# A Conformer block on one core: the sum of the attention output's halves in one reduce or in two, and other constants for the planner

## The chip, the core and the metric

The kernel runs on one core of a Trainium2 chip. Times are device microseconds of one execution of the whole program. Its engines work side by side, each through its own list of instructions in order: PE (matrix multiplies, with PEld for the weight loads), DVE (vector work), ACT (functions such as exp), POOL (small vector work) and SP (issues DMAs). PSUM, where PE writes, has 8 banks of 512 float32 for each of 128 partitions.

## What is computed

Two sequences of 4000 rows of 144 go through one Conformer block: a feed-forward half step, attention with 4 heads of 36, a gated convolution of 5 taps, a second feed-forward half step, and layer norms. The part that matters here is the attention:

```python
qkv = h @ w_qkv                                  # B, T = 2, 4000; 4 heads of 36
scores = jnp.einsum('bhqd,bhkd->bhqk', q, k) * scale
p = _softmax(scores, axis=-1)
att = jnp.einsum('bhqk,bhkd->bhqd', p, v)
att = att.transpose(0, 2, 1, 3).reshape(B, T, D)
x = x + att @ w_o
```

The softmax is taken without a maximum: the exps are summed along with the product with v, by a column of ones beside v, and the division comes at the end.

## The kernel before

**Tiles.** Queries are cut into chunks of 512 (the eighth of each sequence has 416), heads into two pairs. A chunk with a pair of heads is a group; there are 2 x 8 x 2 = 32, in a fixed order. In a group, keys come in 31 tiles of 128 and a rest of 32. For one tile of keys PE computes the scores of both heads into two PSUM banks (tile PS<-QT,KT, four matmuls of 64 x 64 by 512), ACT takes the exp of both in one instruction of 128 x 1024 (PT<-PS), and PE multiplies it with v into banks 4 and 5 (PS<-PT,VA, four matmuls): the upper 64 keys of the tile add up in bank 4, the lower 64 in bank 5. So at the end of a group the attention output lies in two halves that have to be added. The scores use banks 0 to 3 in turn; banks 6 and 7 serve all other work.

**Exp on DVE.** Since ACT is the busiest engine, some exps are computed on DVE by bits: one instruction per head takes the scores from PSUM to an integer that is nearly the exp's bit pattern (PU<-PS), and four more over both heads correct it (`exact`: PF<-PU, PC<-PF, PC<-PC,PF, PU<-PU,PC). Either a whole tile goes this way (`far_tiles`: taken from the far end of the group's list of key tiles, or of the next group's), or one head of a tile goes to ACT and the other to DVE (`emit_exp`, a split tile). PU has 3 buffers (`NPD`), PT has 7 (`NPT`). The outputs of a DVE tile can only be added once its group is the current one and has begun.

**The end of a group.** When the last output matmul of a group is emitted, `output_done` starts `epilogue`. It adds the halves with one DVE tensor_reduce of banks 4 and 5 into OTF (128 x 512 float32), transposes OTF in four pieces of 128 queries on PE into one bank of 6 and 7 (PS<-IDF,OTF), takes the reciprocal of the sums (RD) and multiplies (AN). After the second pair of heads `post1` goes on with the output projection, the convolution and so on. The next group's first output matmul overwrites banks 4 and 5, and so waits for the reduce.

**The order.** There is no fixed schedule in the code. A planner (`Rec`, `Sched`) runs when the kernel is built: it keeps a modelled time for each engine, and each piece of work is a generator that asks for an engine with `need(...)`. `Sched.best` takes the request that can start first by the model; among those within a small window it takes the lowest rank (`free_first` is -1). A request's earliest time is the modelled end of the generator's last instruction, plus the latency `LAT` of its engine (`Sched.advance`, line 260). An instruction that a generator emits without a `need` in front of it comes straight after the one before. The main loop at line 1237 emits scores (`emit_S`), exps (`emit_exp`) and outputs (`emit_pending`); outputs whose exp is not ready, or whose group has not become the current one, are held in a list, and no new scores are emitted when six are held.

**The order constants** stand in `TUNE` (line 342): eight tuples for eight stretches of four groups each. By position: (0) how long after ACT could start may DVE come free for a tile to be split; (1) a far tile is taken from a group only while more than so many key tiles are left in it; (2) how long before POOL comes free the correcting DVE instructions may be planned (`Quiet`); (3) the window in `Sched.best`; (4) with how many tiles left the corrections are hurried.

Of the kernel before, what the change touches and what calls it, by code (L numbers as in the profile page):

```python
# [6 lines left out]
ALU = mybir.AluOpType  # L7
# [30 lines left out]
class Rec:  # L38
# [2 lines left out]


    ENGS = ("pe", "act", "dve", "pool", "sp")
    LAT = dict(pe=0.195, act=0.243, dve=0.152, pool=0.08, sp=3.0)
    NEAR = {("act", "dve"): 0.06, ("dve", "dve"): 0.028, ("pool", "dve"): 0.04}

    def __init__(self, nc):
# [11 lines left out]
    def op(self, eng, name, *a, r=(), w=(), q=None, cost=0.1, kind=None, lat=None, port=False, **k):  # L59
        o = Op()  # L60
        o.eng, o.name, o.a, o.k, o.q = eng, name, a, k, q
        o.deps, o.inc, o.cnt = [], False, 0
        lane = eng if q is None else "q:" + q
        o.idx = self.n.get(lane, 0)
        self.n[lane] = o.idx + 1
        for key in r:
            h = self.hist.setdefault(key, ([], []))
            o.deps += [(d, True) for d in h[0]]
            h[1].append(o)
        for key in w:  # L70
            h = self.hist.setdefault(key, ([], []))
            o.deps += [(d, False) for d in h[0] + h[1] if d is not o]
            if h[1] and not (len(h[1]) == 1 and h[1][0] is o):
                self.hist[key] = ([o], [])
            else:
                h[0].append(o)
        start = self.free[eng]
        for d, raw in o.deps:
            if d.eng != eng or d.q is not None or (raw and eng != "pe"):
                start = max(start, d.done - self.NEAR.get((d.eng, eng), 0.0))  # L80
        if eng == "pe":
            if kind != self.kind:
                start += 0.1
            self.kind = kind
        end = start + cost
        if eng == "pool" and self.run_end > end - 0.05:
            end = self.run_end + 0.13
        if port:
            self.run_end = end
            if self.behind is not None and start < self.free["pool"] - 0.05 < end:  # L90
                p, th = self.behind
                late = end + 0.13 - self.free["pool"]
                self.free["pool"] += late
                p.done += late
                if th is not None:
                    th.ready = max(th.ready, p.done)
        self.free[eng] = end
        o.done = end + (self.LAT[eng] if lat is None else lat) + (0.045 if kind == "q" else 0.0)
        self.last = o.done
        if eng == "pool":  # L100
            self.behind = (o, self.cur)
        self.ops.append(o)
        return o
# [119 lines left out]
def need(eng, slots=None, kids=(), cond=None, rank=None):  # L223
    return (eng, slots, kids, cond, rank)
# [76 lines left out]
def bass_standalone__conformer_family_zipformer__speech_kernel(  # L301
# [21 lines left out]
    def wid(c):  # L323
        return LAST if c % CPB == CPB - 1 else CH
# [4 lines left out]
    R = Rec(nc)  # L329
    op = R.op  # L330
    S = Sched(R)

    def sb(name, shape, dt=BF16):
        return nc.alloc_sbuf_tensor(name, [128] + list(shape), dt)
# [4 lines left out]
    GAP = 0.2  # L339
    MORE = 3  # L340
    HURRY, RELAX = -2, 1
    TUNE = [(0.003, 10, 0.47, 0.032, 3), (0.003, 10, 0.47, 0.032, 3), (0.003, 10, 0.47, 0.032, 3), (0.025, 10, 0.56, 0.065, 3), (0.089, 13, 0.66, 0.057, 3), (0.003, 10, 0.47, 0.032, 3), (0.022, 10, 0.67, 0.039, 3), (0.075, 12, 0.7, 0.063, 3)]
    LEAD = -2
    LAG, LAG_END = 5, 4
    NWARM = 30
# [4 lines left out]
    def tune(i):  # L350


        return TUNE[min(s_grp[0] * len(TUNE) // 32, len(TUNE) - 1)][i]

# [20 lines left out]
    OTF = sb("OTF", [CH], F32)  # L375
# [7 lines left out]
    IDF = sb("IDF", [128], F32)  # L383
# [22 lines left out]
    PSV = PS[:, :].rearrange("p (b n) -> p b n", n=512)  # L406
# [61 lines left out]
    for i in range(NWARM):  # L468
        op("pe", "matmul", PSV[:, i % 8, 0:256], lhsT=DUM[:, 0:128], rhs=DUM[:, :], start=True, stop=True,
           r=["DUM"], w=[("ps", i % 8)], cost=0.213 if i < 24 else 0.109)  # L470
# [51 lines left out]
    def dve_cost(n):  # L522
        return 0.07 + n / 960.0
# [298 lines left out]
    def post1(c, a):  # L822
        b, cc = c // CPB, c % CPB
        tb = wid(c) // NB
        s1 = yield need("pe", xtp)
        s2 = yield need("pe", xtp)

        def half(g):
            yield from transp(AN[0:tb, a, 2 * g:2 * g + 2, :], [("AN", a), "ANP"], c, s1, g)
            yield from residual(  # L830
                c, g, lambda i: [(xt(c, s1, k, i * tb, (i + 1) * tb), WO[0:KROWS[k], k, :]) for k in range(2)], 1.0,
                [("XT", s1, g), "WO"], 0.07)
            yield from ln_tr(c, s2, g)

        kids = S.spawn(half(g) for g in range(2))
        yield need("pe", kids=kids, cond=lambda: c < NUS or c - NUS in conv_done)
        xtp.give(s1)
        anp.give(a)
        kids = S.spawn([glu_a(c, s2), glu_b(c, s2)])
        yield need("pool", kids=kids)  # L840
        xtp.give(s2)
        us, up = c % NUS, (c - 1) % NUS
        if cc == 0:
            op("pool", "memset", UA[:, us, 2:4, 0:1], 0.0, w=[("UL", us)], cost=0.15)
            op("pool", "memset", UB[:, us, 0:1], 0.0, w=[("UL", us)], cost=0.15)
        else:
            for dst, src, w, r in (
                    (UA[:, us, 2:4, 0:1], UA[:, up, 2:4, TB:TB + 1], ("UL", us), ("U", up)),
                    (UB[:, us, 0:1], UB[:, up, TB:TB + 1], ("UL", us), ("U", up)),
                    (UA[:, up, 0:2, TB + 1:TB + 2], UA[:, us, 0:2, 1:2], ("UR", up), ("U", us)),  # L850
                    (UB[:, up, TB + 1:TB + 2], UB[:, us, 1:2], ("UR", up), ("U", us))):
                op("pool", "tensor_copy", dst, src, r=[r], w=[w], cost=0.25)
        if cc == CPB - 1:
            op("pool", "memset", UA[:, us, 0:2, tb + 1:tb + 2], 0.0, w=[("UR", us)], cost=0.15)
            op("pool", "memset", UB[:, us, tb + 1:tb + 2], 0.0, w=[("UR", us)], cost=0.15)
        glu_done.add(c)
# [72 lines left out]
            yield from g  # L929

    an_of = {}

    def epilogue(b, qc, p, gi):
        c = b * CPB + qc
        n, tb = wid(c), wid(c) // NB
        op("dve", "tensor_reduce", out=OTF[:, 0:n], in_=PSV[:, 4:6, 0:n].rearrange("p b n -> p n b"),
           axis=mybir.AxisListType.X, op=ALU.add, r=[("ps", 4), ("ps", 5)], w=["OTF"],
           cost=dve_cost(2 * n))
        bk = yield need("pe", banks)
        for i in range(NB):  # L940
            op("pe", "transpose", PSV[0:tb, bk, i * 128:(i + 1) * 128], OTF[:, i * tb:(i + 1) * tb],
               IDF[:, :], r=["OTF", "IDF"], w=[("ps", bk)], cost=0.122, kind="f")
        if p == 0:
            an_of[c] = yield need("dve", anp)
        yield need("dve", cond=lambda: c in an_of, rank=free_first)
        a = an_of[c]
        v = PSV[0:tb, bk, :].rearrange("p (i h d) -> p i h d", i=NB, h=2)
        op("dve", "reciprocal", RD[0:tb, gi % 2, :, :], v[:, :, :, DH], r=[("ps", bk)], w=[("RD", gi % 2)],
           cost=0.24)
        yield need("dve", rank=free_first)  # L950
        op("dve", "tensor_tensor",
           AN[0:tb, a, :, p * HD:(p + 1) * HD].rearrange("p i (h d) -> p i h d", h=2), v[:, :, :, 0:DH],
           RD[0:tb, gi % 2, :, :].rearrange("p i (h o) -> p i h o", o=1).to_broadcast([tb, NB, 2, DH]),
           op=ALU.mult, r=[("ps", bk), ("RD", gi % 2)], w=[("AN", a)], cost=0.38)
        banks.give(bk)
        if p == 1:
            yield from post1(c, a)
# [100 lines left out]
    def begun_group(gi):  # L1058
        return (gi, 4, 0) in begun or (gi, 4, 1) in begun
# [146 lines left out]
    while len(ff1_done) < CPB or 0 not in kv_done:  # L1206
        t, th = S.best()
        S.run(th)
    banks.restrict([6, 7])
    while banks.held - banks.only:  # L1210
        t, th = S.best()
# [12 lines left out]
    def emit_pending(force=False):  # L1224
        while pend:
            m = pend[0]
            gi = tiles[m][0]
            if gi != o_grp[0]:
                return
            t = exps[m]  # L1230
            if not begun_group(gi):
                t = max(t, R.ready("OTF"))
            if not force and len(pend) < NPT - 2 and t > R.free["pe"] + 0.1:
                return
            emit_O(pend.pop(0))

    while next_tile() is not None or n_e < len(tiles):
        a = s_start() if next_tile() is not None else R.free["pe"]
        full = len(pend) >= NPT - 1
        if full:  # L1240
            emit_pending(force=True)
            full = len(pend) >= NPT - 1
        t, th = S.best()
# [19 lines left out]
        if len(tiles) >= 2 or not more:  # L1263
            emit_exp(n_e)
            emit_pending()
            pend.append(n_e)
            n_e += 1
    while o_grp[0] < len(groups):
        emit_pending(force=True)
        if o_grp[0] < len(groups):  # L1270
            t, th = S.best()
# [7 lines left out]
    while S.threads:  # L1279
        t, th = S.best()  # L1280
# [34 lines left out]
```

## Time and profile before

| | |
|---|---|
| median of 3 unprofiled runs | 934.28 us (934.25 to 934.55) |
| profiled execution | 935.62 us |
| span of its instructions | 933.8 us |
| granted clock of PE | 1.00 throughout |
| HBM traffic | 3.31 MB read, 2.30 MB written |

The profile comes from one execution. Nearly all instructions carry line 163, the planner's helper that emits them, so they are told apart by their tiles: `PT<-PS` writes tile PT from PSUM. A group's row gives the busy time, the mean duration of one in ns, and the idle time of the engine just before them with what ended it. The first reduce of OTF starts at 82 us and the last at 897 us; before lies the first feed-forward part of the first sequence, behind lies what is left of the last chunk. The recorded durations of neighbouring instructions on one engine overlap a little, so where the time from one start to the next matters it is taken from the timeline.

### The profile page before, as it was taken

The page shows a single profiled execution, that of the slowest core. Times are in us where ns is not written, and L with a number is a line of the kernel's source. Part 1 is how long each engine was busy: PE and PEld are TensorE (multiplying, and loading weights), DVE is VectorE, ACT ScalarE, POOL GpSimd, SP SyncE. Part 2 cuts the span into 40 slices and gives each one's busy share as a digit, 9 for nine tenths or more (in the row PEclk, how much of TensorE's full clock was granted, in tenths as well). Part 3 has the DMA queues.
Part 4 walks back from the last instruction along what each step waited for, and adds up shares of the span by engine and source line. Part 5 has one row for each costly group of instructions (what it writes and reads, how often), then busy time and mean ns, then how long its engine had stood idle before and what let it go on. Part 6 is the DMA issues. An engine that isn't in the chain of part 4 may idle for free.

```text
span 933.8 us, 25544 instructions
## 1 busy us (share of the span) xinstructions
PE 860.8 (92%) x10838; PEld 343.0 (37%) x10838; DVE 858.4 (92%) x1975; ACT 884.2 (95%) x1126; POOL 170.8 (18%) x395
## 2 busy tenths in 40 slices
PE   8998899999999998999999999899988999899989
PEld 5633233333243333334343333333323333333447
DVE  8868999999999999999989999999999999898954
ACT  6799999999999999999999999999999999999963
POOL 7500010302111120211211111102202120130223
DMA  5310010103011020201100020101001020101100
GB/s 143 50 21 13 13 25 13 40 8 46 13 28 27 7 52 14 38 16 24 28 8 5 16 36 11 30 7 30 20 1 30 13 42 2 30 18 22 22 19 14
DMA packets 79810, 23.26 MB, mean 25 GB/s; under 512 B 77120, under 2 KB 79696, under 8 KB 79696
## 3 DMA queue, kind: packets, MB, share of 16 engines
q1 hardware_dynamic: 78656, 21.15, 11.6%
q8 instruction: 85, 1.39, 0.7%
q10 hardware_dynamic: 1040, 0.48, 0.2%
q14 instruction: 29, 0.24, 0.1%
HBM read 3.31 MB, written 2.30 MB: 6 GB/s over the span
## 4 chain that ended last, share of the span: by engine, by line
ACT 60%; PE 25%; DVE 13%; DMA 1%; issue 1%; POOL 1%; SPq 0%; ACTq 0%; DVEq 0%
ACT PT L163 52%; PE PS L163 25%; ACT TH L163 5%; DVE PU L163 4%; DVE PC L163 2%; DVE XN L163 1%; DVE ST L163 1%; DVE X L163 1%; ACT HT L163 1%; DVE HT L163 1%; DVE PF L163 1%; DVE OTF L163 1%; ACT PR L163 1%; DMA XT<-XN 0%; POOL RS L163 0%
## 5 line engine op out<-in xcount | busy, mean ns | idle before, releaser
L163 ACT ACTIVATE PT<-PS 128x1024 bf16<-128x1024 f32 (+2 forms) x848 | 795.8, 1067 | 9.7 <-PE PS L163 7.1
L163 PE MATMUL PS<-QT,KT 64*64 64x512 bf16 (+1 forms) x4032 | 431.1, 389 | 49.4 <-ACT PT L163 36.1
L163 PE MATMUL PS<-PT,VA 64*37 64x512 bf16 (+1 forms) x3350 | 327.1, 371 | 0.8 <-ACT PT L163 0.6
L163 PEld LDWEIGHTS PS<-QT,KT 64*64 64x64 bf16 x4032 | 128.2, 103 | 325.2 <-ACT PT L163 199.9
L163 DVE TENSOR_SCALAR PU<-PS 128x512 uint16<-128x512 f32 (+1 forms) x309 | 201.4, 671 | 5.8 <-PE PS L163 4.2
L163 POOL TENSOR_SCALAR RS<-ST 128x2 f32<-128x2 f32 (+1 forms) x160 | 33.2, 208 | 689.8 <-DVE ST L163 688.8
L163 POOL TENSOR_TENSOR RS<-RS,NHALF 128x2 f32<-128x2 f32 (+1 forms) x160 | 122.5, 766 | 13.3
L163 DVE TENSOR_TENSOR PC<-PC,PF 128x1024 bf16<-128x1024 bf16 (+1 forms) x155 | 103.4, 671 | 0.6
L163 DVE TENSOR_TENSOR PU<-PU,PC 128x1024 uint16<-128x1024 uint16 (+1 forms) x155 | 103.4, 669 | 0.2
L163 PEld LDWEIGHTS PS<-PT,VA 64*37 64x37 bf16 x3350 | 96.5, 96 | 13.5 <-ACT PT L163 1.3
L163 DVE TENSOR_SCALAR XN<-X,ST,RS 128x144 bf16<-128x144 bf16 (+1 forms) x312 | 83.2, 311 | 12.9 <-POOL RS L163 11.8
L163 ACT ACTIVATE TH<-PS 128x512 bf16<-128x512 f32 (+2 forms) x135 | 88.7, 657 | 1.9 <-PE PS L163 1.8
L163 PE MATMUL PS<-XT,WA 128*128 128x512 bf16 (+3 forms) x256 | 71.1, 378 | 6.7 <-DVE PU L163 3.4
L163 DVE BATCH_NORM_STATS2 ST<-X 128x6 f32<-128x288 bf16 (+1 forms) x160 | 69.1, 449 | 0.6 <-DMA X<-in_x_dram 0.3
L163 DVE SCALAR_TENSOR_TENSOR HT<-TH,PS 128x512 bf16<-128x512 bf16 (+3 forms) x105 | 64.8, 618 | 3.8 <-ACT TH L163 3.5
L163 PE MATMUL PS<-PU,VA 64*37 64x512 bf16 (+1 forms) x618 | 66.8, 376 | 1.1 <-DVE PU L163 0.8
L163 DVE SCALAR_TENSOR_TENSOR X<-PS,X 128x288 bf16<-128x288 f32 (+1 forms) x128 | 56.1, 450 | 9.9 <-PE PS L163 8.9
L163 DVE TENSOR_SCALAR PC<-PF 128x1024 bf16<-128x1024 uint16 (+1 forms) x155 | 63.0, 411 | 0.3
L163 DVE TENSOR_SCALAR PF<-PU 128x1024 uint16<-128x1024 uint16 (+1 forms) x155 | 62.5, 412 | 0.1
L163 PE MATMUL PS<-WB,HT 128*128 128x144 bf16 (+1 forms) x640 | 56.1, 228 | 2.0 <-ACT HT L163 0.6
L163 PEld LDWEIGHTS PS<-WB,HT 128*128 128x128 bf16 (+1 forms) x640 | 39.7, 101 | 35.3 <-issue 19.3
L163 DVE TENSOR_REDUCE OTF<-PS 128x512 f32<-128x1024 f32 (+1 forms) x32 | 38.4, 1199 | 12.6 <-PE PS L163 12.3
(97 smaller groups left out, 600.5 us busy)
## 6 DMA issues: line engine op xcount, KB each, us to landing
X<-in_x_dram SPq DMA_DIRECT2D x14, 144.0 KB, 3.7
out_dram<-XN SPq DMA_DIRECT2D x28, 72.0 KB, 1.8
XT<-XN SPq DMA_TRANSPOSE x94, 2.5
XT<-AN SPq DMA_TRANSPOSE x28, 2.5
X<-in_x_dram SPq DMA_DIRECT2D x2, 117.0 KB
out_dram<-XN SPq DMA_DIRECT2D x4, 58.5 KB
WA<-in_w_ff1a_dram ACTq DMA_DIRECT2D x1, 144.0 KB, 2.8
WB<-in_w_ff1b_dram ACTq DMA_DIRECT2D x1, 144.0 KB, 3.9
```

The source lines that it names most:

```text
L163: ins = getattr(eng, o.name)(*o.a, **o.k)
```

## The change

The reduce is issued as two, of the first and of the last 256 queries (208 where a chunk has 416), each into its own half of OTF with its own dependency. The second asks for DVE anew. Of the four transposes the first two depend on the first half, the last two on the second, and between the pairs PE is asked for anew. `copied` notes for each group the modelled end of its second reduce, and the next group's outputs are not emitted before that is known. Both reduces still read banks 4 and 5 whole as far as dependencies go, so the next group's outputs wait for both. The constants in `TUNE` and three of the planner's latencies in `LAT` have other values.

```diff
-    LAT = dict(pe=0.195, act=0.243, dve=0.152, pool=0.08, sp=3.0)
+    LAT = dict(pe=0.198, act=0.253, dve=0.149, pool=0.08, sp=3.0)
...
-    TUNE = [(0.003, 10, 0.47, 0.032, 3), (0.003, 10, 0.47, 0.032, 3), (0.003, 10, 0.47, 0.032, 3), (0.025, 10, 0.56, 0.065, 3), (0.089, 13, 0.66, 0.057, 3), (0.003, 10, 0.47, 0.032, 3), (0.022, 10, 0.67, 0.039, 3), (0.075, 12, 0.7, 0.063, 3)]
+    TUNE = [(-0.007, 12, 0.58, 0.045, 3), (-0.017, 13, 0.69, 0.04, 2), (-0.007, 12, 0.58, 0.045, 3), (-0.007, 12, 0.58, 0.045, 3), (-0.007, 12, 0.58, 0.045, 3), (-0.007, 12, 0.58, 0.045, 3), (-0.007, 12, 0.58, 0.045, 3), (-0.007, 12, 0.58, 0.045, 3)]
...
+    copied = {-1: 0.0}
...
-        op("dve", "tensor_reduce", out=OTF[:, 0:n], in_=PSV[:, 4:6, 0:n].rearrange("p b n -> p n b"),
-           axis=mybir.AxisListType.X, op=ALU.add, r=[("ps", 4), ("ps", 5)], w=["OTF"],
-           cost=dve_cost(2 * n))
+        for j in range(2):
+            if j:
+                yield need("dve", rank=free_first)
+            i0, i1 = j * n // 2, (j + 1) * n // 2
+            op("dve", "tensor_reduce", out=OTF[:, i0:i1], in_=PSV[:, 4:6, i0:i1].rearrange("p b n -> p n b"),
+               axis=mybir.AxisListType.X, op=ALU.add, r=[("ps", 4), ("ps", 5)], w=[("OTF", j)], cost=dve_cost(n))
+        copied[gi] = R.last
         bk = yield need("pe", banks)
         for i in range(NB):
+            if i == 2:
+                yield need("pe")
             op("pe", "transpose", PSV[0:tb, bk, i * 128:(i + 1) * 128], OTF[:, i * tb:(i + 1) * tb],
-               IDF[:, :], r=["OTF", "IDF"], w=[("ps", bk)], cost=0.122, kind="f")
+               IDF[:, :], r=[("OTF", i // 2), "IDF"], w=[("ps", bk)], cost=0.122, kind="f")
...
             if not begun_group(gi):
-                t = max(t, R.ready("OTF"))
+                if gi - 1 not in copied:
+                    return
+                t = max(t, copied[gi - 1])
```

## The prediction

> **What bounds the kernel now.** I read the page's engine table and chain first, then the groups of instructions kept apart by shape, the sums over the stretch from 75 to 900 us, what ACT and DVE waited for there, and last the timeline around the ends of groups.
>
> ```profile
> span 933.8 us, 25544 instructions
> PE 860.8 (92%) x10838; PEld 343.0 (37%) x10838; DVE 858.4 (92%) x1975; ACT 884.2 (95%) x1126; POOL 170.8 (18%) x395
> ...
> ACT 60%; PE 25%; DVE 13%; DMA 1%; issue 1%; POOL 1%; SPq 0%; ACTq 0%; DVEq 0%
> ```
>
> Three engines are above 90%, and the chain runs mostly over ACT. The shares hide the start (to about 75 us) and the tail (from 900 us); the sums over what lies between show what is left there.
>
> ```profile
> 75.00:900.00 825.00, 758.90 (x9687) 279.18 (x9686) 784.91 (x1743) 812.53 (x1004) 128.30 (x290) 1.00 0.11 22
> ```
>
> Columns are PE, weight loads, DVE, ACT, POOL, then the granted clock (1.00). In 825 us ACT is busy 812.53, so it idles 12.5 us; DVE idles 40.1 us. ACT is the bound, with DVE close behind as a second server for the same work: an exp is either one ACT instruction or a far tile on DVE.
>
> ```profile
> L163 ACT ACTIVATE PT<-PS 128x1024 bf16<-128x1024 f32 x725 | 703.3, 1101 | 7.7 <-PE PS L163 5.6
> ...
> L163 ACT ACTIVATE PT<-PS 128x512 bf16<-128x512 f32 x15 | 9.7, 649 | 0.5 <-PE PS L163 0.5
> ...
> L163 ACT ACTIVATE PT<-PS 128x416 bf16<-128x416 f32 x6 | 3.1, 524 | 0.3 <-PE PS L163 0.3
> ```
> ```profile
> 108.18 2.92 ACT L163 ACTIVATE PT<-PS 128x1024 bf16<-128x1024 f32 x3
> 111.34 1.02 ACT L163 ACTIVATE PT<-PS 128x1024 bf16<-128x1024 f32 x1 [0.25 <-PE PS L163]
> ```
> ```profile
> L163 DVE TENSOR_SCALAR PU<-PS 128x512 uint16<-128x512 f32 x271 | 179.5, 683 | 5.2 <-PE PS L163 3.6
> L163 DVE TENSOR_TENSOR PC<-PC,PF 128x1024 bf16<-128x1024 bf16 x136 | 92.4, 683 | 0.5
> L163 DVE TENSOR_TENSOR PU<-PU,PC 128x1024 uint16<-128x1024 uint16 x136 | 92.4, 681 | 0.2
> ...
> L163 DVE TENSOR_SCALAR PC<-PF 128x1024 bf16<-128x1024 uint16 x136 | 56.1, 417 | 0.2
> L163 DVE TENSOR_SCALAR PF<-PU 128x1024 uint16<-128x1024 uint16 x136 | 55.7, 418 | 0.1
> ...
> L163 DVE TENSOR_REDUCE OTF<-PS 128x512 f32<-128x1024 f32 x28 | 34.3, 1224 | 8.2 <-PE PS L163 8.0
> ...
> L163 DVE TENSOR_REDUCE OTF<-PS 128x416 f32<-128x832 f32 x4 | 4.1, 1025 | 4.3 <-PE PS L163 4.3
> ```
> ```profile
> 186.26 1.23 DVE L163 TENSOR_REDUCE OTF<-PS 128x512 f32<-128x1024 f32 x1 [0.60 <-PE PS L163]
> 187.40 1.28 DVE L163 TENSOR_SCALAR PU<-PS 128x512 uint16<-128x512 f32 x2
> ...
> 456.51 1.02 DVE L163 TENSOR_REDUCE OTF<-PS 128x416 f32<-128x832 f32 x1 [0.28 <-PE PS L163]
> 457.45 0.58 DVE L163 TENSOR_SCALAR PU<-PS 128x416 uint16<-128x416 f32 x1
> ```
>
> Recorded durations overlap. Three exps in 2.92 us, the last of about 1.10, step by 0.91 each. The reduce of 1.23 is followed after 187.40 - 186.26 = 1.14 us, so about 0.08 of a DVE duration lies under the next one. A far tile therefore costs DVE 2 x 683 + 418 + 417 + 683 + 681 ns less 6 x 0.08, that is 3.08 us, and takes 0.91 us off ACT. **Exchange rate**: 1 us more or less on DVE is worth 0.91/3.08 = 0.30 us on ACT, if the planner keeps both full.
>
> **Where a group ends.** Of ACT's 12.5 us, these views say what it waited for, and how a typical one looks on PE.
>
> ```profile
> ACT PT L163 <- PE PS L163: 7.1, 23, 1.2
> ```
> ```profile
> 617.85 0.60 PE L163 MATMUL PS<-PT,VA 64*37 64x512 bf16 x8
> 618.29 0.38 PE L163 MATMUL PS<-PR,VR 64*37 64x512 bf16 x2
> 618.60 0.66 PE L163 MATMUL PS<-IDF,OTF 128*128 128x128 f32 x4
> 619.19 0.41 PE L163 MATMUL PS<-QT,KT 64*64 64x512 bf16 x4
> ```
> ```profile
> 619.65 1.02 ACT L163 ACTIVATE PT<-PS 128x1024 bf16<-128x1024 f32 x1 [0.25 <-PE PS L163]
> ```
>
> After the reduce PE works off the outputs held back (8 + 2 matmuls), then four float32 transposes of OTF, and only then the scores for which ACT waits. The transposes hold PE for 619.19 - 618.60 = 0.59 us and the stall is 0.25. The same picture stands ahead of 10 of the 23 stalls, from 111.34 to 619.65, with 0.18 to 0.40 us each and 2.7 us together.
>
> **The change, part by part.**
>
> 1. **A second reduce per group.** By the starts, 512 queries cost 1.14 and 416 cost 457.45 - 456.51 = 0.94 us for 1024 and 832 inputs: 1.04 ns an input, 0.07 us fixed. Two halves cost 0.07 us more, 32 groups 2.2 us of DVE, at 0.30 **+0.7 us**. From recorded means the fixed part is 1224 - 1024 x 1.04 = 0.16 us, 5.1 us in all, so +1.5 at the upper end; nothing if DVE's idle 40.1 us takes it in.
>
> [...]
>
> 2. **Transposes in two pieces.** The second pair asks for PE anew, so scores can go between. A pair takes about half of 0.59, 0.29 us, more than the 0.25 stall. I take nine tenths of 2.7 away, **-2.5 us**. The bounds are 0 (the planner puts the pairs next to each other, or the stall passes to the matmuls ahead of them) and -2.7. A second switch between transposes and scores costs PE at most another 0.29 a group; PE has 825.0 - 758.9 = 66 us idle there to hide it.
>
> 3. **The next group's outputs begin later.** The first half is issued at once; the second is a request that the planner sees only when the first one's result is ready, so another DVE instruction (0.34 to 0.60 us by the durations above less the overlap) can go between. The next group's outputs and the second pair of transposes wait for the second half; behind them in PE's order stand scores, and so ACT, and held with them are PT's 7 buffers and PU's 3. One place shows what a long queue costs:
>
> ```profile
> 675.01 1.26 PE L163 MATMUL PS<-PT,VA 64*37 64x512 bf16 x20 [0.22 <-DVE OTF L163]
> 676.10 0.39 PE L163 MATMUL PS<-QT,KT 64*64 64x512 bf16 x4
> ```
> ```profile
> 676.54 1.02 ACT L163 ACTIVATE PT<-PS 128x1024 bf16<-128x1024 f32 x1 [0.38 <-PE PS L163]
> ```
>
> 20 held matmuls take 676.10 - 675.01 = 1.09 us ahead of scores, 0.22 per tile of 4, and ACT loses 0.38. A hold of 0.5 us adds half a tile, 0.11 us, at each of 32 ends: up to 3.5 us. Mostly PE is ahead of ACT, so I take **+0.8**; the lower end is 0.
>
> 4. **Order constants.** The second number rules when far tiles pass to the next group: 10 before (13 in stretch 4, 12 in the last), 12 after, 13 in stretch 1. Finished earlier, they should hold the reduce up less. DVE's wait for PE ahead of the reduce, in stretches 1, 2 and 5 (constant 10) and 4 (13):
>
> ```profile
> DVE OTF L163 <- PE PS L163: 1.8, 4, 0.6
> ```
> ```profile
> DVE OTF L163 <- PE PS L163: 1.0, 3, 0.4
> ```
> ```profile
> DVE OTF L163 <- PE PS L163: 1.5, 3, 0.7
> ```
> ```profile
> DVE OTF L163 <- PE PS L163: 0.4, 2, 0.3
> ```
>
> 4.3 us in 12 groups against 0.4 in 4: 0.26 a group less. In the 24 groups that stood at 10 that would be 6 us of DVE, -1.9 us by the rate. One stretch is thin evidence, so I take **-1.0** (bounds -1.9 and 0).
>
> The first number falls to -0.007 from as much as 0.089: fewer exps are split between ACT and DVE. There are 15 + 6 = 21 split ones. A half left on ACT saves 0.91 - (0.649 - 0.19) = 0.45, as much as half a far tile, so if far tiles take their place it is **0**; if nothing does, +21 x 0.45 = +9.5 us, the worst end. The third (how early a DVE instruction may start behind POOL), the fourth (how wide a choice ranks) and the latencies move the order everywhere without adding work. By DVE's idle 40.1 us at 0.30, a perfect order would bring 12 us; as much as a third of it either way, 4 us, seems possible. I take **0**.
>
> 5. **Tail.** After the last reduce DVE has nothing else to do. The first two transposes run beneath the second half, two instead of four stand behind it: about -0.29 + 0.07, **-0.2**.
>
> Sum: 0.7 - 2.5 + 0.8 - 1.0 - 0.2 = **-2.2 us** on a profiled execution of 935.6 us (its span of 933.8 and 1.8 around it), 933.4 us. The median of the unprofiled runs is 934.28, 1.3 below that execution; there the same sum gives **932.1 us**.
>
> **The rivals.**
>
> *The hold at the group's end decides: slower.* Where the second half is pushed behind another instruction, PU's three buffers stay taken by far tiles of the coming group, which may only be used once that group has begun. If DVE then finds nothing else, it idles for the whole 0.5 us at each of 32 ends, 16 us, at 0.30 +4.8 us in place of +0.8; and if the threshold of 12 fills PU earlier still, the -1.0 falls away. 0.7 - 2.5 + 4.8 - 0.2 = +2.8: **937.1**. It decides once all three buffers are taken at the reduce. For it: DVE is nearly full, so something is always ready to go between. Against it: LN, residuals and gates are there to fill DVE.
>
> *Fewer splits without far tiles in their place: slower.* With half of the 21 replaced, 9.5/2 - 2.2 = +2.6, all lost +7.3: about **938**. For it: far tiles also need one of three buffers and a free bank. Against: split ones are 21 of 848.
>
> *Stalls move, and nothing is gained: no change.* Half of the stalls remain behind the other held matmuls (-1.2), the second reduce costs its upper +1.5, the hold +0.8, the constants give half, -0.5: +0.6, less 0.2 in the tail, **934.7**.
>
> *The new order is better in general.* On top of the -2.2, a fifth of DVE's idle time becomes far tiles, 8 us x 0.30 = -2.4: **929.7**.
>
> **How the numbers follow.** My forecast of 932.1 (own range 930 to 933.5) has 0.42, the hold 0.22, the splits 0.08, no change 0.12, the better order 0.16. A measurement of this kernel can tell about 0.2%, 1.9 us, from no change. Faster: the better order and 0.36 of the forecast's 0.42, 0.52. Within 0.2%: the other 0.06 of it and 0.11 of the no-change case, 0.17. Slower: the rest, 0.31. The range from 927.5 to 938.5 leaves out the far parts of the better order and of the lost splits, some 2 in 10 with the unknown of the re-ordering at both ends.
>
> **What would show it.** Right: 64 reduces of about 0.69 us each; transposes in twos with scores between, and ACT's stalls of 0.25 us behind four transposes gone, so that its wait of 7.1 us for PE falls to about 4.5; DVE's wait ahead of the reduce under 6 us between 75 and 900; 823 to 830 full exps on ACT with fewer splits. Wrong: more full exps than 835; the next group's first output 1 us or more later after the first reduce's start than now; DVE idling over 45 us in the same stretch; or a new ACT stall behind a long row of outputs at the group's end.

## The result, and the profile after

The changed kernel takes 939.98 us (median of 4 runs, 939.53 to 942.3) against 934.41 for the kernel before (4 runs): 1.0062 times as long, 95% interval 1.0049 to 1.0074. It is slower by 0.6%, where 932.1 was forecast, and it lies outside the range of 927.5 to 938.5. The profiled execution took 939.85 us; the page's head and its chain:

```profile
span 938.0 us, 25564 instructions
PE 867.5 (92%) x10839; PEld 344.1 (37%) x10839; DVE 853.3 (91%) x1985; ACT 887.9 (95%) x1131; POOL 171.4 (18%) x395
...
ACT 48%; PE 34%; DVE 15%; POOL 1%; issue 1%; DMA 1%; ACTq 0%; DVEq 0%
```

The span is 4.2 us longer than before. (The medians are 5.6 apart; the profiled execution of before lay 1.2 above its median, that of after 0.1 below.) ACT is busy 3.7 us longer, DVE 5.1 us shorter. The exps by shape, then the ends of the exps in the timelines of before and of after:

```profile
L163 ACT ACTIVATE PT<-PS 128x1024 bf16<-128x1024 f32 x724 | 700.2, 1086 | 7.8 <-PE PS L163 5.7
L163 ACT ACTIVATE PT<-PS 128x832 bf16<-128x832 f32 x104 | 83.6, 912 | 0.6 <-PE PS L163 0.5
L163 ACT ACTIVATE PT<-PS 128x512 bf16<-128x512 f32 x22 | 14.1, 642 | 0.0
L163 ACT ACTIVATE PT<-PS 128x416 bf16<-128x416 f32 x4 | 2.3, 570 | 0.0
```
```profile
887.59 9.29 ACT L163 ACTIVATE PT<-PS 128x832 bf16<-128x832 f32 x12
```
```profile
893.68 7.07 ACT L163 ACTIVATE PT<-PS 128x832 bf16<-128x832 f32 x9
```

Of 32 x 31 = 992 key tiles, 854 now have an exp on ACT, 26 of these split: 138 far tiles and 26 split ones, where there were 144 and 21. Six exps more at 0.91 us, less five halves at 0.45, are 3.2 us of ACT. The exps end at 900.75 instead of 896.88 us, 3.9 later, and the tail is 0.3 longer: that is the 4.2.

So DVE took less of the exps: 6 x 3.08 - 5 x 1.54 = 10.8 us less. What it did with the time, between 75 and 900 us (columns as in the prediction):

```profile
75.00:900.00 825.00, 761.08 (x9656) 277.69 (x9655) 777.63 (x1748) 813.45 (x1007) 128.74 (x290) 1.00 0.11 21
```

DVE idles 825 - 777.63 = 47.4 us in that stretch, 7.3 more than before. Its waits there, before and then after:

```profile
DVE OTF L163 <- PE PS L163: 12.3, 25, 3.5
DVE XN L163 <- POOL RS L163: 6.8, 15, 0.9
DVE PU L163 <- PE PS L163: 4.2, 12, 1.1
DVE HT L163 <- ACT TH L163: 3.5, 8, 1.0
...
DVE X L163 <- PE PS L163: 1.5, 3, 1.2
```
```profile
DVE OTF L163 <- PE PS L163: 8.8, 19, 1.3
DVE XN L163 <- POOL RS L163: 8.4, 18, 0.7
DVE HT L163 <- ACT TH L163: 7.1, 12, 1.9
DVE PU L163 <- PE PS L163: 6.6, 20, 0.9
DVE X L163 <- PE PS L163: 3.8, 7, 1.5
```

Four waits (XN, HT, PU, X) rose by 9.9 us together. The wait ahead of the reduce (OTF) seems to fall by 3.5 us, but that is the edge of the stretch. The last reduce of the program, in before and then in after:

```profile
897.34 1.02 DVE L163 TENSOR_REDUCE OTF<-PS 128x416 f32<-128x832 f32 x1 [3.50 <-PE PS L163]
```
```profile
901.22 1.09 DVE L163 TENSOR_REDUCE OTF<-PS 128x208 f32<-128x416 f32 x2 [1.26 <-PE PS L163]
```

It lies inside the stretch before and behind it after. For the other 31 groups DVE waits 12.3 - 3.5 = 8.8 us before and 8.8 after: nothing was gained there. Taken from 75 us to the end of the exps in each kernel (896.88 and 900.75), DVE idles 38.7 us before and 48.1 after, 9.5 more.

The second reduce takes some of DVE's time too:

```profile
L163 DVE TENSOR_REDUCE OTF<-PS 128x256 f32<-128x512 f32 x56 | 38.4, 686 | 8.2 <-PE PS L163 7.6
L163 DVE TENSOR_REDUCE OTF<-PS 128x208 f32<-128x416 f32 x8 | 4.6, 586 | 2.5 <-PE PS L163 2.5
```

One end of a group in the timelines of after, DVE and then PE:

```profile
410.95 0.69 DVE L163 TENSOR_REDUCE OTF<-PS 128x256 f32<-128x512 f32 x1 [0.54 <-PE PS L163]
411.56 0.68 DVE L163 TENSOR_SCALAR PU<-PS 128x512 uint16<-128x512 f32 x1
412.16 0.68 DVE L163 TENSOR_REDUCE OTF<-PS 128x256 f32<-128x512 f32 x1
412.77 0.69 DVE L163 TENSOR_SCALAR PU<-PS 128x512 uint16<-128x512 f32 x1
```
```profile
413.26 0.82 PE L163 MATMUL PS<-PT,VA 64*37 64x512 bf16 x12
414.01 0.44 PE L163 MATMUL PS<-IDF,OTF 128*128 128x128 f32 x2
414.38 0.41 PE L163 MATMUL PS<-QT,KT 64*64 64x512 bf16 x4
414.62 0.39 PE L163 MATMUL PS<-PT,VA 64*37 64x512 bf16 x4
414.93 0.44 PE L163 MATMUL PS<-IDF,OTF 128*128 128x128 f32 x2
```

A half steps by 0.61 us (411.56 - 410.95), two halves by 1.22 against 1.14: 0.08 more, where 0.07 was worked out. A far tile's first instruction stands between the halves, and twelve outputs of the next group come 2.3 us after the first reduce began. The transposes stand in twos with scores between. At this group's end every local step of the edit is there as described; the sum is not.

### The profile page after: what moved, and what is told of

It reads as the page before. It is cut to its first block, busy times and chain, and to the rows that moved or that the text cites. A ratio compares the mean times of both kernels' runs of the same rounds, so it can differ in the third digit from the quotient of the medians.

```text
span 938.0 us, 25564 instructions
## 1 busy us (share of the span) xinstructions
PE 867.5 (92%) x10839; PEld 344.1 (37%) x10839; DVE 853.3 (91%) x1985; ACT 887.9 (95%) x1131; POOL 171.4 (18%) x395
## 4 chain that ended last, share of the span: by engine, by line
ACT 48%; PE 34%; DVE 15%; POOL 1%; issue 1%; DMA 1%; ACTq 0%; DVEq 0%
ACT PT L163 42%; PE PS L163 34%; DVE PU L163 4%; ACT TH L163 4%; DVE PC L163 2%; DVE XN L163 1%; DVE OTF L163 1%; POOL RS L163 1%; DVE HT L163 1%; DVE ST L163 1%; DVE PF L163 1%; ACT HT L163 1%; DVE X L163 1%; DVE QT L163 1%; DMA XT<-XN 0%
## 5 line engine op out<-in xcount | busy, mean ns | idle before, releaser
L163 ACT ACTIVATE PT<-PS 128x1024 bf16<-128x1024 f32 (+3 forms) x854 | 796.9, 1051 | 8.4 <-PE PS L163 6.2
L163 PE MATMUL PS<-PT,VA 64*37 64x512 bf16 (+1 forms) x3364 | 331.2, 371 | 0.6 <-ACT PT L163 0.6
L163 DVE TENSOR_SCALAR PU<-PS 128x512 uint16<-128x512 f32 (+1 forms) x302 | 198.2, 671 | 8.8 <-PE PS L163 6.6
L163 POOL TENSOR_SCALAR RS<-ST 128x2 f32<-128x2 f32 (+1 forms) x160 | 38.7, 242 | 697.0 <-DVE ST L163 696.4
L163 POOL TENSOR_TENSOR RS<-RS,NHALF 128x2 f32<-128x2 f32 (+1 forms) x160 | 116.3, 727 | 13.3
L163 DVE TENSOR_TENSOR PC<-PC,PF 128x1024 bf16<-128x1024 bf16 (+1 forms) x151 | 100.9, 670 | 0.6
L163 ACT ACTIVATE TH<-PS 128x512 bf16<-128x512 f32 (+2 forms) x135 | 85.7, 635 | 2.3 <-PE PS L163 2.1
L163 PE MATMUL PS<-PU,VA 64*37 64x512 bf16 (+1 forms) x604 | 63.7, 376 | 1.0 <-DVE PU L163 0.7
L163 DVE TENSOR_REDUCE OTF<-PS 128x256 f32<-128x512 f32 (+1 forms) x64 | 43.0, 673 | 10.7 <-PE PS L163 10.1
```

The costliest lines, as they stand in the source:

```text
L163: ins = getattr(eng, o.name)(*o.a, **o.k)
```

## The experiments

Theory H: the edit costs by itself, above all the hold, since the second half stands behind another DVE instruction. Theory B: the order that the planner makes with the other constants is what costs. (Theory A, in the first expectation, is the second reduce's own cost.) Since the planner's modelled end of the program was at hand by now (935.4 for before, 940.3 for the changed kernel), it is given as a number of its own where it helps. It stands beside measured times, not in their place.

**1. The edit at the order of before.** The planner runs as before; then single instructions are moved in the finished lists of the engines, and everything else stays where it was. Nothing can answer to the edit with another plan.

```diff
+    R.reorder(halves, pairs, hold, later)
     R.finish(group_qs=("w0", "w1", "w2"))
```

f1_halves, `R.reorder(True, False, False)`: each reduce becomes two, back to back.

> The planner plans the kernel before as it is; afterwards, with every engine's order kept, each reduce is replaced by two over half of the queries, back to back. Nothing is planned anew. Theory A (the second reduce's own cost, 0.07 to 0.16 us in each of 32 groups, is what matters): 2.2 to 5.1 us of DVE and, with a fixed order that cannot give work to ACT, up to that much on the span: 936.6 to 939.5. Theory B (the order planned anew with the other constants matters): within 2 us of before, 934 to 936.4.

Measured 935.07 against 935.48: ratio 1.000 (0.999 to 1.001). At this order the second reduce itself costs nothing that can be told, at most 0.9 us.

f2_pairs, `R.reorder(False, True, False)`: four scores are moved between the pairs of transposes.

> The kernel before with its order kept, one reduce per group, but in the 29 groups where four score matmuls follow the four transposes, they are moved between the first two and the last two. If the term of -2.5 us of the prediction is right (stalls of 0.25 us of ACT behind four transposes): 931.7 to 932.5. If the stall passes to something else: 934 to 935.

Measured 942.49: ratio 1.0079 (1.0062 to 1.0097), slower by 7 us. The same end of a group on PE in before and in f2_pairs, then on ACT in before and in f2_pairs, then on DVE in f2_pairs:

```profile
188.32 0.66 PE L163 MATMUL PS<-IDF,OTF 128*128 128x128 f32 x4
188.91 0.41 PE L163 MATMUL PS<-QT,KT 64*64 64x512 bf16 x4
189.15 0.39 PE L163 MATMUL PS<-PT,VA 64*37 64x512 bf16 x4
```
```profile
189.38 0.44 PE L254 MATMUL PS<-IDF,OTF 128*128 128x128 f32 x2
189.75 0.41 PE L254 MATMUL PS<-QT,KT 64*64 64x512 bf16 x4
190.09 0.44 PE L254 MATMUL PS<-IDF,OTF 128*128 128x128 f32 x2
190.46 0.40 PE L254 MATMUL PS<-PT,VA 64*37 64x512 bf16 x4
```
```profile
189.37 1.02 ACT L163 ACTIVATE PT<-PS 128x1024 bf16<-128x1024 f32 x1 [0.26 <-PE PS L163]
```
```profile
185.44 6.72 ACT L254 ACTIVATE PT<-PS 128x1024 bf16<-128x1024 f32 x7
```
```profile
190.57 0.21 DVE L254 RECIPROCAL RD<-PS 128x8 f32<-128x8 f32 x1 [0.38 <-PE PS L254]
```

ACT runs seven exps without a gap: the 0.26 us stall of before is gone at this place, as forecast. But four transposes and four scores now take 190.46 - 189.38 = 1.08 us of PE instead of 189.15 - 188.32 = 0.83, and DVE stands still for 0.38 us ahead of RD, which needs the last transpose. In the whole stretch that wait is 9.2 us, against 1.2 before, and ACT's wait for PE ahead of exps has not fallen but risen, from 7.1 us to 9.1:

```profile
ACT PT L254 <- PE PS L254: 9.1, 29, 0.9
```

The 128 transposes keep PE busy for 27.3 us in the whole program, against 20.9 before. What was won at single places was lost again on PE, on DVE and at other places of ACT.

f3_hold, `R.reorder(True, False, True)`: halves, and the next DVE instruction between them.

> As f1_halves, and the second reduce is moved behind the DVE instruction that follows it, in 31 of 32 groups. Theory H (the held second half lets the next group begin late, and that costs 0.5 us per group of DVE or ACT): 937 to 940. Theory B: the held outputs are taken in by the 7 buffers of PT, within 2 us of f1_halves.

Measured 947.86: ratio 1.0124 (1.0100 to 1.0148). Next to f1_halves that is 12.8 us for 31 holds, 0.41 each. Three of its four executions had a granted clock of 0.995 or 0.996, though; the one at 1.00 took 943.75, 8.8 us above the median of f1_halves at that clock (934.96), which is 0.28 us a hold. PE and ACT of f3_hold at the same end of a group:

```profile
188.80 0.41 PE L254 MATMUL PS<-QT,KT 64*64 64x512 bf16 x4 [0.51 <-ACT PT L254]
189.66 0.62 PE L254 MATMUL PS<-PT,VA 64*37 64x512 bf16 x8 [0.45 <-DVE OTF L254]
```
```profile
191.47 1.02 ACT L254 ACTIVATE PT<-PS 128x1024 bf16<-128x1024 f32 x1 [0.89 <-PE PS L254]
```

The next group's outputs were planned to start just then. PE, in order, waits 0.45 us for the second half with the scores behind it, and ACT misses 0.89 us instead of 0.26.

f4_all, `R.reorder(True, True, True)`: all three.

> All three at once at the kept order of before: halves, one DVE instruction between them, scores between the pairs of transposes. Theory H: 937 to 940, as the changed kernel. Theory B: 932 to 936.4, so that the edit without a new plan does not make the kernel 5.6 us slower.

Measured 951.45: 1.0175 (1.0158 to 1.0192). Taken at a granted clock of 1.00, f2_pairs loses 7.2 us against before, f3_hold 9.0 (one execution) and f4_all 16.3: the two add up.

f5_pairs_rd1, `R.reorder(False, True, False, 1)`, and f6_halves_pairs_rd1, `R.reorder(True, True, False, 1)`: RD one place later.

> f2_pairs, and each reciprocal (RD) moved behind the DVE instruction that follows it, in 28 of the 32 groups. In f2_pairs ACT no longer stalled behind the transposes at the ends looked at, but DVE waited 9.2 us for PE ahead of RD (1.2 in before). If that wait at the head of DVE's order is the price of the pairs: 933 to 936. If pairs cost PE or ACT directly: 940 or more, as f2_pairs.

> f5_pairs_rd1 with the reduce in two halves back to back: the whole edit at the kept order of before, with nothing between the halves and RD one place later. As f1_halves cost nothing, the same as f5_pairs_rd1 within 1 us; in any case below the 939.98 of the changed kernel if the new order, not the edit, is what the changed kernel pays for.

Measured 939.4 (1.0056, 1.0041 to 1.0071) and 940.62 (1.0076, 1.0056 to 1.0096). Against the executions of before beside it, f5 loses 5.3 us where f2_pairs lost 7.0: the wait ahead of RD, now 1.6 us, was some 2 us of the price. About 5 us remain. The extra PE time at the group's end is what is left to explain them, but no run takes it away by itself; this expectation was half a miss. f6 was to lie within 1 us of f5 and below the 939.98 of the changed kernel; it lies 1.2 above f5 and 0.6 above the changed kernel. Theory H seemed to win here: the pairs and the hold cost several us each. But a kept order shows only what a plan loses when a piece of it is moved. The next step turns this around.

**2. The edit undone at the order of the changed kernel.** The same tool on the changed kernel, in the other direction.

```diff
+    R.reorder(join, group)
     R.finish(group_qs=("w0", "w1", "w2"))
```

> The changed kernel's own order kept, but in the 31 groups where another DVE instruction stands between the two reduces, the second is put directly behind the first; the instruction between comes after both. Theory H (the hold makes the changed kernel slow): outputs of the next group are released 0.3 to 0.6 us sooner, 935 to 938. If the planner had already put other work where the hold is: within 1 us of the changed kernel, 939 to 941.

> The changed kernel's own order kept, but in the 27 groups where other matmuls stand between the pairs of transposes, the first pair is moved down to the second. If the pairs' extra switches on PE (about 0.25 us a group by the trace of f2_pairs, 7 us of PE in all) reach ACT: 935 to 938. If PE has room for them there: 939 to 941; more than 941 if the burst of four stalls ACT as in before.

> Both at once in the changed kernel's order: reduces back to back, four transposes together, far tiles and everything else as planned with the new constants. If the two edits cost what the changed kernel lost: 934 to 936. If the order and its 6 fewer far tiles (6 exps more on ACT at 0.91 us) cost it: 938 to 941.

Measured against 934.28 of before: u1_after_join, `(True, False)`, 948.35 (1.0155, 1.0131 to 1.0180); u2_after_four, `(False, True)`, 939.77 (1.0060, 1.0044 to 1.0076); u3_after_both, `(True, True)`, 949.16 (1.0151, 1.0134 to 1.0168). Removing the hold does not give its price back; it costs another 8 us (7 at a granted clock of 1.00, 946.65 against 939.7), which none of the expectations of u1 and u3 had. DVE of u1_after_join at the group's end shown above for after, and PE:

```profile
414.71 1.29 DVE L225 TENSOR_REDUCE OTF<-PS 128x256 f32<-128x512 f32 x2 [0.54 <-PE PS L225]
415.92 0.68 DVE L225 TENSOR_SCALAR PU<-PS 128x512 uint16<-128x512 f32 x1
417.10 0.69 DVE L225 TENSOR_SCALAR PU<-PS 128x512 uint16<-128x512 f32 x1 [0.50 <-PE PS L225]
```
```profile
416.66 0.62 PE L225 MATMUL PS<-QT,KT 64*64 64x512 bf16 x6 [0.38 <-DVE PU L225]
```

The far tile's PU, which stood between the halves, now comes 0.60 us later behind the first reduce (1.21 instead of 0.61), so its PSUM bank comes free later: PE waits 0.38 us for it with the next scores, and DVE waits 0.50 us for those. In the stretch its wait ahead of PU is 11.8 us against 6.6. Grouping the transposes again (u2) changes nothing that can be told, as its expectation had it for a PE with room there: PE is busy 2.0 us less in the stretch, and ACT's wait ahead of exps is 6.6 us, against 6.2. So neither piece, taken out of this order, gives the 5.6 us back.

**3. Code and constants exchanged.** Both are planned anew.

```diff
-    LAT = dict(pe=0.195, act=0.243, dve=0.152, pool=0.08, sp=3.0)
+    LAT = dict(pe=0.198, act=0.253, dve=0.149, pool=0.08, sp=3.0)
```

(c3_old_code_new_latencies: this line alone in the kernel before; c2_old_code_new_constants: with the new TUNE too; c1_new_code_old_constants: the changed code with both lines of before.)

> The changed code with TUNE and LAT of before, planned anew. Theory B (the order decides, and constants fit only the code they stand with): slower than both, since the planner's own modelled end is 950.5 (935.4 for before, 940.3 for the changed kernel): 948 to 952. Theory H (the edit costs by itself, the constants little): 939 to 941, as the changed kernel. If the constants alone made the changed kernel slow: 932 to 935.

> The code of before with TUNE and LAT of the change. Theory B: as slow as the changed kernel, modelled end 940.5: 939 to 942. Theory H: the edit is not in it, so about as before, 933 to 936.

> The code and TUNE of before; only the three latencies in LAT are those of the change (0.003, 0.010 and 0.003 us apart). Theory B: any small move of the planner's numbers throws away the order of before; modelled end 952.2: 949 to 954. Theory H, and the prediction, which gave LAT nothing: 934 to 936.

Measured against 935.66: c1 949.84 (1.0158, 1.0136 to 1.0179), c2 938.62 (1.0037, 1.0024 to 1.0050), c3 947.50 (1.0127, 1.0112 to 1.0142). c1 came as theory B had it; c2 and c3 lie 0.4 and 1.5 us below its ranges, and above those of theory H. Three latencies that stand in the planner's model alone, in no instruction, moved by 0.003 to 0.010 us, cost 1.3%: twice what the whole change did. With both sets of constants exchanged but the old code, c2, 0.37% of the loss is there without the edit; DVE's idle time in the stretch is then 45.4 us already, and two waits that the prediction had not priced, ahead of PU and of X, have grown from 4.2 and 1.5 us:

```profile
75.00:900.00 825.00, 757.24 (x9669) 280.06 (x9668) 779.58 (x1729) 814.03 (x1008) 132.27 (x290) 1.00 0.12 22
```
```profile
DVE OTF L163 <- PE PS L163: 12.8, 20, 4.0
DVE PU L163 <- PE PS L163: 9.1, 21, 1.1
...
DVE X L163 <- PE PS L163: 4.6, 11, 0.7
```

The wait ahead of the reduce has not fallen here either: of its 12.8 us, 4.0 belong to the last reduce and 8.8 to the other 31.

The code's part under these constants is the difference, 0.25% (by the two intervals some 0.1 to 0.4), and by c1 it is 1.6% under the old ones. The price of the edit is whatever the constants beside it make of it. How wide that may go, by the planner's modelled end over the same 100 random sets of constants for both codes (one set of TUNE for all stretches; us). Neither the sets nor the ranges they were drawn from are on record, so this table illustrates and proves nothing:

```
code      mean    spread (sd)   lowest   pairwise difference
before    947.9   4.3           941.2
changed   949.8   5.7           937.2    +1.9 (standard error 0.6)
```

In it a set drawn at random is 12 us worse than the kernel before, whose 935.4 lies below all hundred of its code.

**4. Each code with constants of its own.** For both codes, and for one reduce with transposes in pairs, constants were sought in the planner alone, step by step and stretch by stretch, keeping what ended earlier.

```diff
-    LAT = dict(pe=0.198, act=0.253, dve=0.149, pool=0.08, sp=3.0)
+    LAT = dict(pe=0.1923, act=0.2386, dve=0.1533, pool=0.08, sp=3.0)
...
-    TUNE = [(-0.007, 12, 0.58, 0.045, 3), (-0.017, 13, 0.69, 0.04, 2), ...
+    TUNE = [(0.036, 13, 1.09, 0.054, 2), (0.053, 13, 0.68, 0.046, 4), ...
```

(That of s4_new_code_searched against the changed kernel; s0_old_code_searched and s3_pairs_only_searched differ in the same two lines.)

> The changed code, with other values in TUNE and LAT, found by trying some 1500 sets in the planner alone and keeping the one with the earliest modelled end, 931.4. If the edit costs by itself (the hold, the second reduce, the pairs): not below the 939.98 of the changed kernel by more than 2. If the constants made the changed kernel slow: 930 to 934, at or below before.

> The code of before with constants found in the same way and with the same number of tries; modelled end 931.6. If the edit is neutral once each code has constants of its own: within 2 us of s4_new_code_searched. If the edit costs 1 to 2 us: 1 to 2 us below it.

> One reduce, but the transposes in two pieces, constants found in the same way; modelled end 930.9, with 138 far tiles and 29 split ones (144 and 21 in before, 138 and 26 in the changed kernel). If the 6 far tiles fewer are what made the changed kernel slow: about 938. If the number of far tiles says little by itself: 930 to 933.

Measured against 934.52: s4 934.23 (0.9999, 0.9988 to 1.0009), s0 935.58 (1.0011, 0.9999 to 1.0022), s3 934.46 (1.0005, 0.9995 to 1.0016). All three take what the kernel before takes. **The changed code is not slower by itself; with the constants that came with it, it was.** s4 and the changed kernel differ in nothing but the two lines, and stand 5.7 us apart. s3 has as few far tiles as the changed kernel, 138, and is not slow: their number is a symptom. What pays for them is ACT's wait for PE, in the same stretch of s3, of s4 and then of after:

```profile
ACT PT L163 <- PE PS L163: 3.6, 11, 1.0
```
```profile
ACT PT L163 <- PE PS L163: 3.4, 13, 0.6
```
```profile
ACT PT L163 <- PE PS L163: 6.2, 21, 1.2
```

s4 has 852 exps on ACT, four more than before at 0.91 us (less three halves at 0.45), and stalls 3.7 us less ahead of them than the 7.1 of before: more than the pairs of transposes were to bring is there, and what DVE gave up takes most of it back. That it is the pairs that bring it is likely, but not shown: s0, without pairs, waits 7.1 us, but c2, without pairs too, 4.5.

By the medians no version beat the kernel before. They hide one thing. Of s4's 11 executions only two had a granted clock of 1.00, and these took 931.72 and 932.14 us; the 24 of the kernel before at that clock, run beside them, have a median of 934.2, and none is below 933.63. At 0.998 it is 934.0 (3 executions) against 936.3 (5). At the same clock s4 is about 2.2 us faster; its median loses that again, as 9 of its 11 executions were below 1.00, against 5 of the 29 of before. Why that is so, no run here shows. s0 and s3 do not gain at 1.00 (934.1 and 934.05).

```
planner's modelled end beside the measured median, us
before 935.4 / 934.4    c2 940.5 / 938.6    s4 931.4 / 934.2
after  940.3 / 940.0    c1 950.5 / 949.8    s0 931.6 / 935.6
                        c3 952.2 / 947.5    s3 930.9 / 934.5
```

The model, asked beforehand, would have put the change at +4.9 us, of which 5.6 were measured. It tells fast plans from slow ones, but does not rank the four fastest.

## Why the prediction was wrong

The sign went wrong at part 4. With the old code the new constants cost 0.37%, 3.5 us (c2), where the prediction had -1.0. Under these constants the edit costs another 0.25%, 2.3 us, where parts 1, 2, 3 and 5 had -1.2 together. This split holds for these constants alone: with those of before the same edit costs 1.6% (c1).

1. **Second reduce**, +0.7 us: not contradicted. A half lasts 0.686 us (0.69 was named), two step 0.08 us more, and f1_halves shows no cost beyond 0.9 us, so it cannot tell +0.7 from nothing. The fixed part of 0.16 us by recorded means, from which its upper end of +1.5 came, does not show between neighbours: by the starts two halves cost 0.07 us (u1_after_join) to 0.08 us (after) more than the whole.

2. **Transposes in pairs**, -2.5 us: at the kept order the step that failed is the cover, "PE has 825.0 - 758.9 = 66 us idle there to hide it". That idle time is spread over the stretch (0.5 to 4.2 us in each 25 us of before), and only 1.2 us of it stand directly ahead of the 128 transposes; at the ends shown PE is working off held outputs there. The stall does go at the place shown, but the pairs take 0.25 us more of PE there, and RD, planned for four transposes, waits (9.2 us in the stretch). At that order this was 7 us, not -2.5. In the changed kernel, planned with the pairs, the stalls behind the transposes do go: ten of 2.7 us together before, two of 0.5 after. But new ones stand elsewhere, and ACT's wait falls only from 7.1 to 6.2 us. Scores (64 x 64, bf16) and transposes (128 x 128, float32) differ in shape and in type, and no run shows which of the two, if either, costs the 0.25 us. The prediction had bounded the second switch between them by 0.29 us a group, rightly, and then took it as hidden.

3. **The hold**, +0.8 us: mis-sized for a plan that does not expect it. 0.11 us for a half tile of queue was the step; f3_hold shows 0.28 us an end at a granted clock of 1.00 (0.41 by the median), since PE waits in order (0.45 us at the end shown) and scores stand behind. In the changed kernel the planner expects the hold and fills it, and u1_after_join shows that it can no longer be taken out without loss. From a group's first reduce to the next group's first output it takes 1.4 us in the median of 31 groups before and 2.2 after. s4 has the same hold in its code and is not slow (934.23 us): the hold does not cost by itself. The rival of the hold (937.1) had the sign right, but not the cause: joining the halves did not help.

4. **Order constants**, -1.0 us: this step decided the sign. Its -1.0 rested on reduces that wait less for far tiles, and they do not: 8.8 us for the same 31 groups in before, in c2 and in after. The rest was taken as 0, with 4 us either way, because the other numbers "move the order everywhere without adding work". With the old code the new constants cost 0.37%, about 3.5 us, instead of bringing 1.0; the three latencies alone, with the other constants of before, cost 1.27%, 11.9 us, far outside the 4. In the changed kernel's order DVE waits 9.5 us more up to the end of the exps and takes 6 whole tiles fewer off ACT. Nor were there fewer split exps: 26, where there were 21. The threshold at the first position fell; why more tiles were split all the same is not shown. The rival of the lost splits (938) came nearest to 939.98, but by luck: its cause, fewer splits, did not come.

5. **Tail**, -0.2: it is 0.3 longer.

Of the signs named beforehand as showing the prediction wrong, one came: DVE idling over 45 us (47.4). Of those of being right, the reduces of 0.69 us, the pairs with scores between and 828 full exps came; ACT's wait of about 4.5 us (6.2), DVE's wait under 6 us ahead of the reduce (8.8) and fewer splits did not. What stays open: which numbers of TUNE lose most in the changed kernel, and how much of the 0.25% between c2 and the changed kernel is the edit and how much another accident of order. The random sets, +1.9 us on the average, point to some of it being the edit, but in the planner's model alone.

## What to carry to other kernels

Where instructions are ordered by a planner at build time, a change of code and a change of its constants must be tried apart: here three latencies moved by 0.01 us or less cost twice what the whole change did, and c3 and c1 suggest that a tuned kernel stands at a lucky end of a wide spread. If the planner models the end, ask it first: it had +4.9 of the 5.6 us. Compare medians of versions only after a look at the granted clock of their executions. Price an edit against the engine's idle time at its own place, not over the stretch, and name the next instruction in order on each engine that waits for it. To learn what an edit costs, move it alone in a kept order in both directions; if both lose, it is the plan that is being paid for.

## What was not expected of the hardware

Two float32 transposes of 128 x 128 between scores of 64 x 64 hold PE 0.37 us (189.75 - 189.38 in f2_pairs), where four hold it 0.59: almost two thirds of the time for half of the work. On DVE, two halves back to back cost 0.07 us more than the whole (415.92 - 414.71 = 1.21 in u1_after_join, against 1.14), and 32 such splits nothing that 10 runs could tell. And half a per cent of granted clock shows in the time: s4 took 931.7 to 932.1 us at 1.00 and 935.8 to 936.6 at 0.995.
